# A fused attention and two-layer kernel on one core: the rational function's denominator moves from POOL to ACT and DVE, and the second token block goes from f32 to three f16 passes

## The chip, the cores and the metric

The kernel runs on one core of one Trainium2 chip. Its time is the device time of one execution in microseconds (us), and smaller is better. Five engines work side by side, each through its own instruction queue in order, and wait for each other by semaphores: PE (matrix multiply; its weight loads are shown apart as PEld), DVE (vector), ACT (activation functions), POOL (the general-purpose engine), and SP, which here issues all transfers. A measurement of this kernel can tell about 1% from no change.

## The reference

Three stages follow each other on 4608 tokens (8 batches of 576):

```
p_packed = softmax(p k^T / 8) v          # 32 packed rows a head, 8 heads of 64
x        = softmax(q p_packed^T / 8) p_packed
h = x @ w_in                             # 512 -> 2048
P = a0 + a1 h + a2 h^2 + a3 h^3
Q = 1 + |b0| |h| + |b1| h^2
y = (P / (Q + 1e-6)) @ w_out             # 2048 -> 512
h2 = y @ w_in2                           # 512 -> 1024
solu = h2 * softmax(h2)
out = ((solu - mean) / sqrt(var + 1e-6) * g_ln) @ w_out2
```

All is in f32. The four weights come as 64-bit floats, 25 MB, and are turned into f32 on the chip with integer operations on DVE.

## The kernel before, in words

The tokens are worked off in 9 blocks of 512. For each block there are 16 steps i, one for each 128 of the 2048 hidden columns:

- `m_h` multiplies on PE into one of two PSUM banks (tile `h`). Attention is folded in: `a_pw` makes `pw` (packed rows times w_in) once a batch, and `m_h` multiplies the attention weights `at` with it.
- `elem` (line 678) computes the rational function of that bank. ACT takes |h| into `u` (L690). POOL makes `s` = b1 u + b0 (L335, called at L691), and then `s` = s u (L692); that is the denominator without its 1. ACT makes the numerator's inner part `B` (L693), DVE goes on with it (L694, L695; both read `h` in PSUM). ACT takes Ln and Exp of the denominator (L696, L697), which gives its reciprocal, and DVE does one Newton step and the product (L698, L699, L701 or L703; all their inputs are in SBUF).
- `m_y` multiplies the result `g` with w_out into `Y`, four PSUM banks (tiles `P`).

After the 16 steps `y_out` evicts Y as two f16 halves into `ybig` (ACT L728, DVE L729), twice 128x1024. Then for each quarter t of the block `s_h2` multiplies with w_in2, `s_sm`, `s_lt` and `s_ln` do softmax, transposes by DMA and statistics, and `s_out` multiplies with w_out2.

Precision has two forms. A plain f32 matmul, or both operands split into a high and a low f16 part and three f16 matmuls (`PASS`, line 659) accumulated. `NRAW = 2` (line 204): the first two blocks' `m_y` and the first two batches' `m_h` are f32; the others are in three f16 passes. With f16, `elem` ends in one more step: ACT casts `g`'s high part (L704) and POOL subtracts for the low part (L705). `w_split` (line 454) turns w_out, w_in2 and w_out2 into two f16 parts in place: ACT the high part (L457), DVE the low part (L458). Since the f32 form reads w_out in place, its splits follow block 1's `m_y`, the last that needs f32.

Early on the weights must also be loaded and decoded (`w_decode`, three DVE operations a piece, L399 to L401, 24 pieces), and column sums give bounds that set the f16 scales (`w_bound`, `w_scale`, and `a_scale`, a chain of some 30 one-column operations, mostly on POOL, for each block).

The order on each engine is written by a planner (`Plan`). Every operation has a due time, 16 a block plus an entry of the table `DUE`, and a cost; a list scheduler goes through time with these costs and puts on each engine the earliest due operation that is ready. On the chip nothing is left of the plan but the order on each queue and the semaphores. Buffers are few: 3 each of `s`, `u`, `B` and `g`, 2 banks of `h`, and one PSUM pair that `s_h2`, `a_pw` and the attention share.

## Time and profile before

| | |
|---|---|
| time, median of 3 runs | 1197.74 us (1196.11 to 1203.66) |
| the profiled execution | 1202.27 us, its span 1200.4 us |
| PE busy | 1115.8 us (93%) |
| DVE busy | 976.8 us (81%) |
| ACT busy | 762.0 us (63%) |
| POOL busy | 706.3 us (59%) |
| mean granted clock of PE | 0.983 |

Busy is the time in which at least one instruction of the engine runs. Matmuls overlap each other and their ends are modelled, so how fast PE goes is read from the distance of their starts. A line can be a helper's: every matmul is recorded at L329 and every POOL operation on one tensor at L335, so they are told apart by their tiles. An f32 matmul stands in the trace as two records.

### The profile page before, as it was taken

The page shows a single profiled execution, that of the slowest core. Times are in us where ns is not written, and L with a number is a line of the kernel's source. Part 1 is how long each engine was busy: PE and PEld are TensorE (multiplying, and loading weights), DVE is VectorE, ACT ScalarE, POOL GpSimd, SP SyncE. Part 2 cuts the span into 40 slices and gives each one's busy share as a digit, 9 for nine tenths or more (in the row PEclk, how much of TensorE's full clock was granted, in tenths as well). Part 3 has the DMA queues.
Part 4 walks back from the last instruction along what each step waited for, and adds up shares of the span by engine and source line. Part 5 has one row for each costly group of instructions (what it writes and reads, how often), then busy time and mean ns, then how long its engine had stood idle before and what let it go on. Part 6 is the DMA issues. An engine that isn't in the chain of part 4 may idle for free.

```text
span 1200.4 us, 17951 instructions
## 1 busy us (share of the span) xinstructions
PE 1115.8 (93%) x6549; PEld 529.7 (44%) x6550; DVE 976.8 (81%) x1477; ACT 762.0 (63%) x1256; POOL 706.3 (59%) x931
## 2 busy tenths in 40 slices
PE   4678989999999999999999998999999999999998
PEld 1133344444444454444544454444444444444443
DVE  5987999999978978888878887888788886788633
ACT  3556666676856667567756766577656666667624
POOL 0163847554658647676666655765675865867612
PEclk9698999999999999999999999999999999999999
DMA  9664033110222121311231114111311121211123
GB/s 342 224 230 161 7 123 99 36 53 1 54 77 67 27 54 55 88 27 28 62 109 27 27 40 131 27 27 27 117 28 27 27 53 28 53 27 27 27 53 88
DMA packets 108120, 83.54 MB, mean 70 GB/s; under 512 B 78208, under 2 KB 88576, under 8 KB 108032
## 3 DMA queue, kind: packets, MB, share of 16 engines
q1 hardware_dynamic: 108032, 82.40, 24.4%
q8 instruction: 51, 0.84, 0.3%
q14 instruction: 37, 0.30, 0.1%
HBM read 54.07 MB, written 9.44 MB: 53 GB/s over the span
## 4 chain that ended last, share of the span: by engine, by line
PE 47%; DVE 23%; POOL 13%; ACT 9%; issue 5%; DMA 2%; SPq 0%; DVEq 0%; ACTq 0%; POOLq 0%
PE P L329 37%; PE h L329 9%; POOL s L692 4%; POOL cf L335 3%; DVE B L699 3%; POOL s L335 2%; DVE s L698 2%; POOL g L705 2%; ACT u L696 2%; DVE B L694 2%; DVE B L695 2%; POOL d L335 1%; DVE w L401 1%; DMA lbig<-lbig 1%; DVE at L629 1%
## 5 line engine op out<-in xcount | busy, mean ns | idle before, releaser
L329 PE MATMUL P<-g,w 128*128 128x512 f16 (+1 forms) x1600 | 423.4, 414 | 0.7 <-DVE ybig L729 0.7
L329 PE MATMUL h<-at,pw 128*128 128x192 f16 (+11 forms) x1408 | 235.4, 315 | 8.3 <-ACT at L646 3.2
L335 POOL TENSOR_SCALAR s<-u,aba 128x512 f32<-128x512 f32 x130 | 137.6, 1058 | 173.7 <-ACT u L690 150.9
L329 PEld LDWEIGHTS <-w 128*128 128x128 f16 x1440 | 138.4, 98 | 167.5 <-issue 12.1
L329 PE MATMUL P<-w,ybig 128*128 128x512 f16 x864 | 193.9, 381 | 9.0 <-DVE pw L539 2.5
L705 POOL TENSOR_TENSOR g<-B,g 128x512 f16<-128x512 f32 x112 | 144.2, 1287 | 80.9 <-ACT g L704 76.6
L692 POOL TENSOR_TENSOR s<-s,u 128x512 f32<-128x512 f32 x130 | 186.3, 1433 | 7.0
L329 PE MATMUL P<-w,lbig 128*128 128x512 f16 x768 | 173.0, 379 | 4.9 <-DVE pw L539 2.9
L335 POOL TENSOR_SCALAR d<-d 128x1 f32<-128x1 f32 x216 | 85.3, 395 | 156.6 <-ACT E L790 73.1
L696 ACT ACTIVATE u<-s,lnb 128x512 f32<-128x512 f32 x130 | 93.8, 721 | 98.4 <-POOL s L692 97.9
L698 DVE SCALAR_TENSOR_TENSOR s<-s,u 128x512 f32<-128x512 f32 x130 | 109.2, 840 | 47.8 <-ACT u L697 47.0
L329 PEld LDWEIGHTS <-ybig 128*128 128x128 f16 x864 | 84.7, 98 | 114.2 <-issue 16.0
L329 PEld LDWEIGHTS <-pw 128*128 128x128 f16 x1152 | 101.6, 98 | 64.5 <-issue 13.3
L329 PEld LDWEIGHTS <-lbig 128*128 128x128 f16 x768 | 74.6, 98 | 92.6 <-issue 8.1
L694 DVE SCALAR_TENSOR_TENSOR B<-h,cf,B 128x512 f32<-128x512 f32 x112 | 83.0, 741 | 27.5 <-ACT B L693 27.3
L693 ACT ACTIVATE B<-h,cf 128x512 f32<-128x512 f32 x112 | 86.6, 773 | 21.5 <-POOL g L705 21.5
L699 DVE SCALAR_TENSOR_TENSOR B<-B,cf,u 128x512 f32<-128x512 f32 x101 | 98.2, 972 | 0.0
L697 ACT ACTIVATE u<-u,lnb 128x512 f32<-128x512 f32 x133 | 95.6, 719 | 2.0
L690 ACT ACTIVATE u<-h,cf 128x512 f32<-128x512 f32 x101 | 68.9, 682 | 39.9 <-PE h L329 38.1
L695 DVE SCALAR_TENSOR_TENSOR B<-B,cf,h 128x512 f32<-128x512 f32 x112 | 82.8, 739 | 1.5
L704 ACT CAST g<-B 128x512 f16<-128x512 f32 x112 | 68.6, 613 | 21.6 <-PE P L329 16.9
L703 DVE SCALAR_TENSOR_TENSOR B<-s,B 128x512 f32<-128x512 f32 x98 | 81.0, 827 | 1.1
(144 smaller groups left out, 1469.3 us busy)
## 6 DMA issues: line engine op xcount, KB each, us to landing
w<-in_w_in_dram SPq DMA_DIRECT2D x10, 1024.0 KB, 9.2
kq<-in_kT_dram SPq DMA_DIRECT2D x8, 1152.0 KB, 6.2
w<-in_w_out_dram SPq DMA_DIRECT2D x9, 1024.0 KB, 8.1
kq<-in_qT_dram SPq DMA_DIRECT2D x9, 1024.0 KB, 5.4
out_dram<-w SPq DMA_DIRECT2D x36, 256.0 KB, 2.4
...
```

The source lines that it names most:

```text
L329: nc.tensor.matmul(out=o, lhsT=lhsT, rhs=rhs, start=start, stop=stop)
L335: gp.tensor_scalar(out=o, in0=i, scalar1=s1, scalar2=s2, op0=o0, **({"op1": o1} if o1 else {}))
L692: pool(due, c_pool(512, 2), lambda: gp.tensor_tensor(out=T(s_), in0=T(s_), in1=T(u_), op=ALU.mult), [u_, s_], [s_])
L693: sc(due, c_act(512, 163), lambda: act.activation(out=T(B_), in_=T(h_), func=AF.Identity, scale=coef(17), bias=coef(16)), [h_, *R], [B_], ...
L694: dve(due, c_dve(512), lambda: stt(out=T(B_), in0=T(h_), scalar=coef(14), in1=T(B_), op0=ALU.mult, op1=ALU.mult), [h_, B_, *R], [B_])
L695: dve(due, c_dve(512), lambda: stt(out=T(B_), in0=T(B_), scalar=coef(15), in1=T(h_), op0=ALU.subtract, op1=ALU.mult), [h_, B_, *R], [B_])
L696: sc(due, c_act(512, 105), lambda: act.activation(out=T(u_), in_=T(s_), func=AF.Ln, scale=2.0 ** -40, bias=lnb[:, 0:1]), [s_, "lnb"], [u_])
L697: sc(due, c_act(512, 105), lambda: act.activation(out=T(u_), in_=T(u_), func=AF.Exp, scale=-1.0, bias=lnb[:, 1:2]), [u_, "lnb"], [u_])
L698: dve(due, c_dve(512, 140), lambda: stt(out=T(s_), in0=T(s_), scalar=1.0 + 1e-6, in1=T(u_), op0=ALU.add, op1=ALU.mult), [s_, u_], [s_])
L699: dve(due, c_dve(512, 240), lambda: stt(out=T(B_), in0=T(B_), scalar=coef(18), in1=T(u_), op0=ALU.subtract, op1=ALU.mult), [B_, u_, *R], [B_])
L703: dve(due, c_dve(512, 95), lambda: stt(out=T(B_), in0=T(s_), scalar=2.0, in1=T(B_), op0=ALU.subtract, op1=ALU.mult), [s_, B_], [B_])
L705: pool(due, (1250, 1290), lambda: gp.tensor_tensor(out=T(g_)[:, 1, :], in0=T(B_), in1=T(g_)[:, 0, :], op=ALU.subtract), [B_, g_], [g_])
```

## The change

- `elem`: the denominator no longer goes through POOL. ACT squares h into `s` (scaled by the block's factor, coefficient 14) and takes |h| times b0 into `u` (a new coefficient 22, made by one more one-column POOL operation a block from block 1 on), and DVE joins them: s = b1 s + u, both inputs in SBUF. The old way stays in the code behind `Q_POOL`, which is false for all blocks.
- `NRAW` is 1: block 1, and the second batch, go in three f16 passes. So block 1's `elem` has the cast on ACT and the subtraction on POOL (`LO_POOL` is true throughout), the second batch's `pw` and `at` are split, and w_out's 16 splits follow block 0's `m_y`.
- `w_split` of w_out: ACT makes the high part and then scales the f32 row in place, and POOL subtracts (`LOW_POOL`); DVE has no part in it. The other two weights are split as before.
- The planner: other costs, a rule that DVE operations marked `port` aren't planned beside a POOL operation, and a new table `DUE` with entries for single weight pieces and for blocks 0, 1 and 8. Nothing of these three is executed, but they set the order.

```diff
-    NRAW = 2
+    NRAW = 1
+    LOW_POOL = {1: 1, 2: 0, 3: 0}
+    Q_POOL = lambda j, i: False
+    LO_POOL = lambda j, i: True
...
         sc(due, c_act(512, 100), lambda: act.activation(out=spl[w][:, c, 0, :], in_=raw[w][:, c + 1, :], func=AF.Copy, scale=s), [b, ("wst", w)], [a])
+        if LOW_POOL[w]:
+            sc(due, c_act(512, 100), lambda: act.activation(out=raw[w][:, c + 1, :], in_=raw[w][:, c + 1, :], func=AF.Copy, scale=s), [b, ("wst", w), a], [b])
+            pool(due, (1117, 1157), lambda: gp.tensor_tensor(out=spl[w][:, c, 1, :], in0=raw[w][:, c + 1, :], in1=spl[w][:, c, 0, :], op=ALU.subtract), [a, b], [a, ("spl", w, c)])
+            return
...
-        sc(due, c_act(512, 65), lambda: act.activation(out=T(u_), in_=T(h_), func=AF.Abs, scale=coef(14)), [h_, *R], [u_], [(u_, "u"), (s_, "s")])
-        pool(due, c_pool(512), lambda: ps_(T(s_), T(u_), aba[:, 5:6], aba[:, 4:5], ALU.mult, ALU.add), [u_, "ab"], [s_])
-        pool(due, c_pool(512, 2), lambda: gp.tensor_tensor(out=T(s_), in0=T(s_), in1=T(u_), op=ALU.mult), [u_, s_], [s_])
...
+            sc(due, c_act(512, 65), lambda: act.activation(out=T(s_), in_=T(h_), func=AF.Square, scale=coef(14)), [h_, *R], [s_], [(s_, "s")])
+            sc(due, c_act(512, 65), lambda: act.activation(out=T(u_), in_=T(h_), func=AF.Abs, scale=coef(22)), [h_, *R], [u_], [(u_, "u")])
+            dve(due, c_dve(512), lambda: stt(out=T(s_), in0=T(s_), scalar=aba[:, 5:6], in1=T(u_), op0=ALU.mult, op1=ALU.add), [u_, s_, "ab"], [s_], port=True)
...
+                        if n in self.port and port_at > now:
+                            held.append((due, n))
+                            continue
```

Two places show how the order moves. The first is POOL's queue from its first operation on data, in block 0 of the program. Before, it begins with the denominators of the first steps (L335 and L692 in turn; `aba` holds |a| and |b|):

```order
L335 TENSOR_SCALAR s_85<-u_87,aba 128x512
L692 TENSOR_TENSOR s_85<-s_85,u_87 128x512
L335 TENSOR_SCALAR s_86<-u_88,aba 128x512
L692 TENSOR_TENSOR s_86<-s_86,u_88 128x512
L335 TENSOR_SCALAR s_85<-u_87,aba 128x512
L692 TENSOR_TENSOR s_85<-s_85,u_87 128x512
```

Now it begins with the scale of w_out, the first split of w_out (L483) and the chain of block 0's coefficients:

```order
L358 TENSOR_SCALAR wst<-wst 128x1 x2
L483 TENSOR_TENSOR w_75<-w_75 128x512
L358 TENSOR_SCALAR wst<-wst 128x1 x2
L358 TENSOR_SCALAR cf_117<-pmx 128x1
L358 TENSOR_SCALAR cf_117<-cf_117,wst 128x1
L358 TENSOR_SCALAR cf_117<-cf_117,aba 128x1 x2
```

No denominator is left on POOL; `w_75` is w_out.

The second place is DVE around the second eviction of Y (block 1's, into `ybig`). The rows with `cf_119` are elementwise work of block 2 that stands ahead of it or around it (`cf_118` holds block 1's coefficients). Before:

```order
L698 SCALAR_TENSOR_TENSOR s_85<-s_85,u_87 128x512
L458 SCALAR_TENSOR_TENSOR w_75<-w_75,wst 128x512
L699 SCALAR_TENSOR_TENSOR B_89<-B_89,cf_119,u_87 128x512
L703 SCALAR_TENSOR_TENSOR B_89<-s_85,B_89 128x512
L694 SCALAR_TENSOR_TENSOR B_90<-h_83,cf_119,B_90 128x512
L695 SCALAR_TENSOR_TENSOR B_90<-B_90,cf_119,h_83 128x512
L729 SCALAR_TENSOR_TENSOR ybig<-P_80,cf_118,ybig 128x2x512
L729 SCALAR_TENSOR_TENSOR ybig<-P_81,cf_118,ybig 128x2x512
```

Now (L725 is the join, L765 the eviction):

```order
L728 SCALAR_TENSOR_TENSOR B_90<-B_90,cf_119,h_84 128x512
L731 SCALAR_TENSOR_TENSOR s_85<-s_85,u_87 128x512
L732 SCALAR_TENSOR_TENSOR B_89<-B_89,cf_119,u_87 128x512
L725 SCALAR_TENSOR_TENSOR w_75<-w_75,aba,w_76 128x512
L736 SCALAR_TENSOR_TENSOR B_89<-s_85,B_89 128x512
L731 SCALAR_TENSOR_TENSOR s_86<-s_86,u_88 128x512
L765 SCALAR_TENSOR_TENSOR ybig<-P_80,cf_118,ybig 128x2x512
L765 SCALAR_TENSOR_TENSOR ybig<-P_81,cf_118,ybig 128x2x512
```

Ahead of this eviction stood 22 operations of block 2's `elem` on DVE, and now 11 stand there, three of them joins; the splits of w_out (L458), of which one shows there, are on POOL now. On PE the work ahead of it is the same in both, but for three steps of block 2's `m_h` in place of five.

## Rows read from the trace of the kernel before

**Rows 1.** The profile's page: the span, and the busy time, share of the span and instructions of each engine.

```profile
span 1200.4 us, 17951 instructions
PE 1115.8 (93%) x6549; PEld 529.7 (44%) x6550; DVE 976.8 (81%) x1477; ACT 762.0 (63%) x1256; POOL 706.3 (59%) x931
```

**Rows 2.** The view by windows, five stages of the span: the length, the busy time of each engine (with instructions), the granted clock of PE, the share of the DMA engines, GB/s.

```profile
0.00:120.00 120.00, 80.90 (x487) 31.98 (x489) 93.41 (x136) 63.98 (x122) 35.07 (x25) 0.86 0.68 239
120.00:198.00 78.00, 70.87 (x372) 30.36 (x372) 74.59 (x115) 51.13 (x92) 50.71 (x62) 0.98 0.25 80
198.00:331.00 133.00, 129.88 (x534) 61.71 (x533) 128.15 (x196) 94.09 (x157) 75.35 (x93) 1.00 0.14 38
331.00:990.00 659.00, 627.43 (x4174) 311.38 (x4173) 545.98 (x831) 430.32 (x691) 430.92 (x599) 1.00 0.21 52
990.00:1200.00 210.00, 206.70 (x988) 94.33 (x986) 134.70 (x202) 122.46 (x197) 114.27 (x155) 1.00 0.20 43
```

**Rows 3.** The timeline of DVE at the first and the second eviction of Y: start in us, duration in us, engine, line, operation, tiles, count.

```profile
195.77 2.48 DVE L729 SCALAR_TENSOR_TENSOR ybig<-P,cf,ybig 128x1024 f16<-128x1024 f32 x2 [0.30 <-ACT ybig L728]
...
328.80 2.47 DVE L729 SCALAR_TENSOR_TENSOR ybig<-P,cf,ybig 128x1024 f16<-128x1024 f32 x2
```

**Rows 4.** The timeline of PE in two stretches without idle time: block 1 with f32 (`P<-g,w` is `m_y`, the `h` row is two steps of `m_h`), and a later one with f16 (`P<-w,lbig` is the last multiply, of the same shape as `m_y`).

```profile
261.53 7.13 PE L329 MATMUL P<-g,w 128*128 128x512 f32 x16
268.50 7.03 PE L329 MATMUL P<-w,E 128*128 128x512 f32 x16
275.37 4.17 PE L329 MATMUL h<-at,pw 128*128 128x64 f32 x16
279.38 3.60 PE L329 MATMUL P<-g,w 128*128 128x512 f32 x8
...
415.42 5.34 PE L329 MATMUL P<-w,lbig 128*128 128x512 f16 x24
420.59 1.47 PE L329 MATMUL h<-at,pw 128*128 128x192 f16 x12
```

**Rows 5.** The groups of DVE's instructions from 0 to 331 us, shapes apart: count, busy us, mean ns of one, idle us before them and what ended it.

```profile
L699 DVE SCALAR_TENSOR_TENSOR B<-B,abc,u 128x512 f32<-128x512 f32 x32 | 29.1, 910 | 0.0
L458 DVE SCALAR_TENSOR_TENSOR w<-w,wst 128x512 f16<-128x512 f32 x32 | 26.8, 843 | 0.0
L701 DVE SCALAR_TENSOR_TENSOR g<-s,B 128x512 f32<-128x512 f32 x32 | 22.7, 709 | 0.0
L539 DVE SCALAR_TENSOR_TENSOR pw<-P,bnd,pw 128x1024 f16<-128x1024 f32 x4 | 5.1, 1278 | 0.5 <-ACT pw L538 0.5
```

**Rows 6.** The timelines of DVE and POOL in two stretches of block 8's elementwise work: in the first POOL works on two tensors, in the second its timeline shows nothing from 1063.9 to 1069.5 us.

```profile
1048.56 0.68 DVE L698 SCALAR_TENSOR_TENSOR s<-s,u 128x512 f32<-128x512 f32 x1
1049.16 1.75 DVE L699 SCALAR_TENSOR_TENSOR B<-B,cf,u 128x512 f32<-128x512 f32 x1
...
1048.70 1.66 POOL L692 TENSOR_TENSOR w<-w,u 128x512 f32<-128x512 f32 x1
...
1067.18 0.74 DVE L699 SCALAR_TENSOR_TENSOR B<-B,cf,u 128x512 f32<-128x512 f32 x1
1067.96 0.68 DVE L703 SCALAR_TENSOR_TENSOR B<-s,B 128x512 f32<-128x512 f32 x1
```

**Rows 7.** The timeline of all engines in block 0 (idle time before an instruction, and what ended it, in brackets).

```profile
77.41 10.88 POOL L335 TENSOR_SCALAR s<-u,aba 128x512 f32<-128x512 f32 x1 [3.73 <-DVE g L701]
...
89.67 0.72 ACT L696 ACTIVATE u<-s,lnb 128x512 f32<-128x512 f32 x1 [10.12 <-POOL s L692]
...
93.13 0.59 PE L329 MATMUL P<-w,ones 128*32 128x512 bf16 x1 [9.54 <-ACT pw L534]
...
96.35 0.28 DVE L332 TENSOR_SCALAR p<-P,sum 128x64 f32<-128x64 f32 x1 [8.02 <-PE P L329]
```

**Rows 8.** Groups of the whole span, from the profile's page, with the same columns as rows 5: what POOL does in `elem`, and ACT's |h|.

```profile
L335 POOL TENSOR_SCALAR s<-u,aba 128x512 f32<-128x512 f32 x130 | 137.6, 1058 | 173.7 <-ACT u L690 150.9
L705 POOL TENSOR_TENSOR g<-B,g 128x512 f16<-128x512 f32 x112 | 144.2, 1287 | 80.9 <-ACT g L704 76.6
L692 POOL TENSOR_TENSOR s<-s,u 128x512 f32<-128x512 f32 x130 | 186.3, 1433 | 7.0
L690 ACT ACTIVATE u<-h,cf 128x512 f32<-128x512 f32 x101 | 68.9, 682 | 39.9 <-PE h L329 38.1
```

**Rows 9.** The groups of DVE's instructions from 331 to 990 us.

```profile
L699 DVE SCALAR_TENSOR_TENSOR B<-B,cf,u 128x512 f32<-128x512 f32 x76 | 73.3, 965 | 0.0
L698 DVE SCALAR_TENSOR_TENSOR s<-s,u 128x512 f32<-128x512 f32 x75 | 66.0, 880 | 28.1 <-ACT u L697 28.0
L694 DVE SCALAR_TENSOR_TENSOR B<-h,cf,B 128x512 f32<-128x512 f32 x86 | 63.7, 740 | 19.6 <-ACT B L693 19.4
L757 DVE SCALAR_TENSOR_TENSOR E<-P,d,E 128x1024 f32<-128x1024 f32 x22 | 28.1, 1279 | 16.6 <-ACT E L752 16.5
L750 DVE TENSOR_REDUCE d<-P 128x1 f32<-128x1024 f32 x22 | 26.8, 1218 | 10.2 <-PE P L329 10.2
```

**Rows 10.** The groups of PE's instructions from 331 to 990 us.

```profile
L329 PE MATMUL P<-g,w 128*128 128x512 f16 x1032 | 236.8, 379 | 0.2 <-DVE ybig L729 0.2
L329 PE MATMUL P<-w,ybig 128*128 128x512 f16 x538 | 121.5, 382 | 7.2 <-DVE at L627 2.3 <-DVE pw L539 2.3 <-DVE p L332 1.4
L329 PE MATMUL P<-w,lbig 128*128 128x512 f16 x528 | 119.4, 379 | 4.9 <-DVE pw L539 2.9 <-DVE E L757 1.2 <-DVE pmx L359 0.4
```

More of the change, by code (lines that the diff above doesn't have):

```diff
@@ L50, in __init__, with add @@
         self.parts, self.last_w, self.readers, self.users, self.kind, self.place = [], {}, {}, {}, {}, {}
-        self.slots, self.held, self.pace = {}, {}, {}
+        self.slots, self.held, self.pace, self.port = {}, {}, {}, set()
     def hold(self, key, slot):
         self.kind[key], self.held[key] = None, slot
-    def add(self, eng, due, cost, fn, r=(), w=(), new=(), pace=None):
+    def add(self, eng, due, cost, fn, r=(), w=(), new=(), pace=None, port=False):
         n = len(self.parts)
+        if port or eng == "POOL":
+            self.port.add(n)
         if pace is not None:
@@ L100, in order @@
                 heapq.heappush(ready[p[0]], (p[1], n))
-        out, now, events, pace = [], 0.0, [], 0.0
+        out, now, events, pace, port_at = [], 0.0, [], 0.0, 0.0
         bytes_free = 0.0
@@ L138, in order @@
                     free_at[eng] = now + occ
+                    if got in self.port:
+                        port_at = now + occ
                     if eng == "SP":
@@ L299, in c_pool @@
     def c_pool(n, tensors=1):
-        lat = (2.4 * n + 220) if tensors > 1 else (1.3 * n + 330)
+        lat = (2.14 * n + 175) if tensors > 1 else (0.94 * n + 290)
         return lat - 40, lat
@@ L314, in pe, with dve @@
         plan.add("PE", due, c_pe(mms), run, r, w, new, pace)
-    def dve(due, cost, fn, r=(), w=(), new=()):
-        plan.add("DVE", due, cost, fn, r, w, new)
+    def dve(due, cost, fn, r=(), w=(), new=(), port=False):
+        plan.add("DVE", due, cost, fn, r, w, new, port=port)
     def sc(due, cost, fn, r=(), w=(), new=()):
@@ L398, in w_decode @@
         ov = flat(o.bitcast(U32))
-        dve(due, c_dve2(1024), lambda: v_.tensor_scalar(out=ov, in0=H, scalar1=3, scalar2=0x3FFFFFFF, op0=ALU.logical_shift_left, op1=ALU.bitwise_and), keys, ok)
-        dve(due, c_dve(1024, 0), lambda: v_.scalar_tensor_tensor(out=ov, in0=L, scalar=29, in1=ov, op0=ALU.logical_shift_right, op1=ALU.bitwise_or), keys + ok, ok)
-        dve(due, c_dve(1024, 0), lambda: v_.scalar_tensor_tensor(out=ov, in0=H, scalar=0xC0000000, in1=ov, op0=ALU.bitwise_and, op1=ALU.bitwise_or), keys + ok, ok)
+        dve(due, c_dve2(1024), lambda: v_.tensor_scalar(out=ov, in0=H, scalar1=3, scalar2=0x3FFFFFFF, op0=ALU.logical_shift_left, op1=ALU.bitwise_and), keys, ok, port=True)
+        dve(due, c_dve(1024, 0), lambda: v_.scalar_tensor_tensor(out=ov, in0=L, scalar=29, in1=ov, op0=ALU.logical_shift_right, op1=ALU.bitwise_or), keys + ok, ok, port=True)
+        dve(due, c_dve(1024, 0), lambda: v_.scalar_tensor_tensor(out=ov, in0=H, scalar=0xC0000000, in1=ov, op0=ALU.bitwise_and, op1=ALU.bitwise_or), keys + ok, ok, port=True)
         a = t.bitcast(BF16)
@@ L628, in a_s2 @@
         dve(d, c_dve(1024, 0), lambda: v_.tensor_reduce(out=rA(), in_=X3(), axis=AX.X, op=ALU.max), [x_], [rk], [(rk, "r32")])
-        dve(d, c_dve(1024, 0), lambda: v_.tensor_tensor(out=X3(), in0=X3(), in1=bc(rA()), op=ALU.subtract), [x_, rk], [x_])
+        dve(d, c_dve(1024, 0), lambda: v_.tensor_tensor(out=X3(), in0=X3(), in1=bc(rA()), op=ALU.subtract), [x_, rk], [x_], port=True)
         sc(d, c_act(1024, 0), lambda: act.activation(out=X(), in_=X(), func=AF.Exp, scale=0.125), [x_], [x_])
@@ L639, in a_s2 @@
         dve(d, (262, 344), lambda: v_.reciprocal(out=rB(), in_=rB()), [rk], [rk])
-        dve(d, c_dve(1024, 0), lambda: v_.tensor_tensor(out=X3(), in0=X3(), in1=bc(rB()), op=ALU.mult), [x_, rk], [x_])
+        dve(d, c_dve(1024, 0), lambda: v_.tensor_tensor(out=X3(), in0=X3(), in1=bc(rB()), op=ALU.mult), [x_, rk], [x_], port=True)
         dve(d, c_dve(1024, 20), lambda: v_.transpose(out=T(yk), in_=X()), [x_], [yk], [(yk, "E")])
@@ L649, in a_s2 @@
                 dve(d, c_dve(2 * n, 0), lambda a=a, t=t, n=n: v_.tensor_tensor(out=a()[:, 1, :, :], in0=Y()[:, :, t:t + n], in1=a()[:, 0, :, :], op=ALU.subtract),
-                    [yk, ("a", j, t)], [x_, ("a", j, t)])
+                    [yk, ("a", j, t)], [x_, ("a", j, t)], port=True)
     def piece(j, t, n, b):
@@ L774, in s_lt @@
         sc(due, c_act(1024, 20), lambda: act.activation(out=l[:, 0, 0, :], in_=T(E), func=AF.Copy, scale=2.0 ** 13), [E], [R, *old])
-        dve(due, c_dve(1024, 0), lambda: v_.scalar_tensor_tensor(out=l[:, 0, 1, :], in0=T(E), scalar=2.0 ** 13, in1=l[:, 0, 0, :], op0=ALU.mult, op1=ALU.subtract), [E, R], [(R, 1)])
+        dve(due, c_dve(1024, 0), lambda: v_.scalar_tensor_tensor(out=l[:, 0, 1, :], in0=T(E), scalar=2.0 ** 13, in1=l[:, 0, 0, :], op0=ALU.mult, op1=ALU.subtract), [E, R], [(R, 1)], port=True)
         for a in range(2):
```

33 lines of the change are left out of this document (21 added, 12 removed), and 20 rows, old and new, of the table DUE.

## The prediction

> **What bounds the kernel now.** I read the page first, then the windows, then DVE's and PE's timelines where the windows change. On the page PE is busy for 93% of the span and DVE for 81% [rows 1], which hides that two stages have different limits. In the windows [rows 2] PE has 39.1 us of idle time before 120 us (120 less 80.90), 7.1 and 3.1 in the next two stages, 31.6 from 331 to 990, and 3.3 in the last 210 us. DVE is the other way round: from 120 to 331 us it works 202.7 of 211 us, from 331 to 990 it has 113 us to spare. So from about 20 us to 331 us the weights' decoding and two blocks' elementwise work keep **DVE** at its limit, and afterwards **PE** sets the time. The seam is the second eviction of Y, which ends at 331.3 us [rows 3]; 869.1 us of the span follow it.
>
> The span is 1200.4 us, the profiled execution 1202.27, the median of the runs 1197.74. My sums are differences against the profiled span, and I take them off the median.
>
> **PE's saving.** f32 `m_y` in block 1: 16 records take 268.50 - 261.53 = 6.97 us, so one step (8 records, 4 matmuls) takes 3.49 us. In f16, 24 matmuls take 420.59 - 415.42 = 5.17 us, so 12 take 2.59 [rows 4]. That saves 0.90 x 16 = 14.4 us. Two f32 steps of `m_h` take 279.38 - 275.37 = 4.01 us; six f16 passes of 512 columns take 1.29 us by the same row, and 1.5 with the 64 columns of block 1 that stay f32. That saves 0.5 x 16 = 8.0. Together **22 us of PE work**, all ahead of the seam, where DVE is the limit. Behind the seam PE's work is the same but for two steps of `m_h` more: the order puts three ahead of the eviction in place of five, +2.6 us.
>
> **DVE up to the seam.** It was busy for 93.41 + 74.59 + 128.15 = 296.2 us and idle for 34.8 [rows 2]. Instructions that follow each other overlap by 0.08 us (1048.56 + 0.68 against the next start at 1049.16 [rows 6]), so I take 0.08 off each duration.
> - The join reads two tensors in SBUF, as L701 does (mean 709 ns [rows 5]); undisturbed, L703 takes 0.68 [rows 6]. I take 0.62 us, since L701 ran in the same blocks: 32 x 0.62 = +19.8. The upper end is L699's mean of 965 [rows 9], 0.885: +28.3.
> - w_out's splits leave DVE: 16 x (0.843 - 0.08) [rows 5] = -12.2.
> - The second batch's `pw` gets its low part on DVE: 4 x (1.278 - 0.08) [rows 5] = +4.8. The low part of `at` for 896 columns of block 1 and 256 of block 2, by L701's rate: +1.4. Five more one-column operations for block 1's scales, at most 0.28 each (the row at 96.35 [rows 7]): +1.
> - The order: 22 operations of block 2 stood ahead of the eviction, 11 do now. By L694 (0.740 - 0.08 [rows 9]): -7.3.
> - Idle time. At 77.41 a POOL operation of a denominator took 10.88 us, while DVE ran on; ACT then waited 10.12 us for POOL, PE 9.54 us for ACT, and DVE at last 8.02 us for PE [rows 7]. With no denominator on POOL this chain is gone: -8. I add -2 for the smaller waits of the same kind, by judgement.
> - The port. DVE's work on two SBUF tensors grows when POOL works on two tensors at the same time: L699 took 1.75 us with L692 beside it and 0.74 with POOL idle [rows 6]. L692 goes, but 16 splits of w_out and 16 low parts of block 1 come to POOL, also on two tensors. That is 32 for the 37 steps that had run, so I take -1. The Trainium skill (GPSIMD Engine Reference, Specifications) says that POOL shares its SBUF interfaces with VectorE and that DVE instructions with two SBUF inputs contend; L699's two rows agree, and by the rule alone every join would count at the disturbed 0.885, which makes the sum below +5.0 in place of -3.5.
>
> Sum: 19.8 - 12.2 + 4.8 + 1.4 + 1 - 7.3 - 10 - 1 = **-3.5 us**. So the seam moves little, and most of PE's 22 us become idle time. ACT doesn't decide: it was busy 209 of 331 us, and gets 32 squares of at most 0.682 [rows 8] and some 32 operations for casts and splits, together 44 us.
>
> **Behind the seam.** Here PE sets the time, and `m_y` never waits for `g` (0.2 us in 1032 matmuls [rows 10]). So a shorter chain in `elem` (two ACT operations and a join in place of one and two on POOL of 1.06 and 1.43 us [rows 8]) gives nothing by itself. What PE waits for is DVE, late with `pw`, `at`, `E` and small columns, in 12.1 us of the two groups shown and 31.6 us in all. DVE gets 86 joins (as many as L694 has rows [rows 9]): +53. It loses waiting behind POOL's L692: of POOL's 112 + 130 operations on two tensors on the page [rows 8] the 130 go, about half; L699's excess is 76 x (0.965 - 0.74) = 17 us and L698's 75 x (0.88 - 0.68) = 15, and with L703's a little less I take 23 us back. So DVE goes from 546 to 576 of 659 us, 87%: no limit on average. For PE I take 10 of its 35 us of idle time as won, between nothing and 20: the stretched operations stand in the chains that PE waits for (L629, L649 and L699 all read two SBUF tensors), and POOL comes to the short operations of the statistics sooner. This is the least certain term, and the +2.6 above is set against the waits that a PE two steps behind no longer has.
>
> Forecast: 1197.7 - 3.5 - 10 = **1184 us**.
>
> **The rivals.**
> *A, PE's saving comes through.* DVE's idle time up to the seam shrinks from 34.8 to the 12 or so of the first transfers, because many of its small waits hung on POOL, and the new order fills them; then the seam comes up to 22 us earlier, and behind it the 10 us are won: 1198 - 32 = 1166. For it: DVE's first 120 us hold 26.6 of its idle time, of which the chain at 77 us explains only 8. Against it: DVE had 8.3 us idle in the 211 us after, so it must be the early part alone.
>
> *B, the port takes it back.* In the first two blocks DVE works without a gap, and POOL's splits and low parts meet it; the joins cost 0.885, and the new POOL operations are held up as the one at 77.41 was, now ahead of `m_y` of block 1, which didn't need POOL before. Joins +8.5, no idle time won +10, no gain behind the seam +10: 1184 + 28 = 1212, or 1203 if only the joins and the gain behind the seam fail. For it: 1.75 us of L699 beside L692 against 0.74 without [rows 6]. Against it: POOL's work on two tensors falls by half, and L701 kept 709 ns in these blocks.
>
> *C, DVE becomes the limit behind the seam.* It has 113 us to spare in 659, but 28.1 of it are waits of L698 for ACT, 19.6 of L694, 16.6 of L757, 10.2 of L750 [rows 9], together 74.5. If these stay, only 38.5 us are free, 0.45 us for each of 86 steps; from there on each further 0.1 us a step costs 8.6 us. I have 0.62 a join less 23/86 = 0.27 won back, 0.35, which is under it. At 0.885 with nothing won back it is 0.435 over: 86 x 0.435 = 37 us, 1198 - 3.5 + 37 = 1232, slower. For it: the join stands in DVE's queue between two operations that wait for ACT. Against it: waits shrink when an engine gets fuller, and ACT no longer waits for POOL.
>
> *D, the change doesn't reach POOL.* It does: the order has no denominator there.
>
> **The numbers.** Forecast 0.50, from 1174 to 1197; A 0.24; B 0.16; C 0.10. Under 1% is what a measurement here can't tell from no change, so faster means below 1185.8 and slower above 1209.7. Of the forecast I give 0.28 to faster and 0.22 to no change; A is faster; B gives 0.11 to no change and 0.05 to slower; C is slower. So faster 0.52, no change 0.33, slower 0.15. The range from 1162 to 1208 leaves out C, half of B's upper value and the lowest part of A.
>
> **What will show it.** Right: the second eviction of Y ends between 318 and 331 us; PE's idle time ahead of it is longer by some 18 us; POOL is busy for about 390 us (706 less 359 of denominators, 1.433 + 1.058 for each of 144 steps, plus 32 x 1.29 [rows 8]); the join's mean lies between 0.69 and 0.80 us; PE's idle time behind the seam falls to about 25 us. A is right if the eviction ends before 312; B if the join's mean is above 0.9 or a POOL split is held for over 3 us and PE waits for it; C if DVE is busy for over 92% from the seam to 990 us and PE waits for `g`. I am wrong in principle if the time changes without the seam or PE's idle time behind it having moved.

## The result, and the profile after

The changed kernel takes **1162.94 us** (median of 4 runs, 1162.42 to 1163.76) against 1200.2 us for the kernel before in the same measurement: ratio 0.9691, 95% interval 0.9654 to 0.9728. That is 37 us faster, where 14 were forecast. The profiled execution took 1162.42 us, its span is 1160.6. One execution each of a1_old_plan and a2_old_ops below took far longer than the rest, 2932.52 and 1953.92 us; without it their medians are 1232.64 and 1183.46.

The page's span and busy line, and the view by windows for the stretches that answer to [rows 1, 2] (the seam now lies at 318 us):

```profile
span 1160.6 us, 18141 instructions
PE 1090.8 (94%) x6678; PEld 519.6 (45%) x6678; DVE 1002.0 (86%) x1616; ACT 851.1 (73%) x1432; POOL 418.7 (36%) x696
...
0.00:120.00 120.00, 82.04 (x537) 31.43 (x538) 102.76 (x160) 77.38 (x143) 19.64 (x40) 0.90 0.67 239
120.00:198.00 78.00, 65.33 (x342) 29.01 (x340) 76.93 (x116) 68.03 (x121) 30.54 (x31) 0.95 0.20 72
198.00:318.00 120.00, 113.64 (x596) 54.82 (x597) 115.00 (x189) 96.73 (x164) 53.98 (x80) 0.98 0.17 46
318.00:950.00 632.00, 623.86 (x4205) 310.37 (x4202) 555.52 (x912) 472.26 (x781) 248.51 (x429) 1.00 0.23 56
950.00:1160.00 210.00, 205.90 (x1006) 93.94 (x1004) 151.75 (x244) 136.69 (x226) 66.01 (x118) 1.00 0.21 40
```

DVE's timeline at the second eviction of Y, to be held against [rows 3]:

```profile
314.53 0.68 DVE L731 SCALAR_TENSOR_TENSOR s<-s,u 128x512 f32<-128x512 f32 x1
315.13 2.47 DVE L765 SCALAR_TENSOR_TENSOR ybig<-P,cf,ybig 128x1024 f16<-128x1024 f32 x2
```

It ends at 317.6 us in place of 331.3, so 13.7 us are won ahead of the seam. From there to the end of the span it is 843.0 in place of 869.1: **26.1 us are won behind it**. PE's idle time behind the seam is 8.1 + 4.1 = 12.2 us by the windows; before it was 31.6 + 3.3 = 34.9. So nearly all of what was won there is time in which PE had waited.

What PE waited for shows in the view of waits (engine, tile and line that waited, what it waited for; us in total, times, longest). Before, from 331 to 990 us:

```profile
PE P L329 <- DVE E L757: 5.7, 4, 2.8
PE P L518 <- DVE p L332: 5.7, 5, 1.6
PE P L329 <- DVE pw L539: 5.2, 6, 2.0
...
PE P L329 <- DVE at L627: 2.3, 1, 2.3
PE h L329 <- DVE at L649: 2.1, 2, 1.6
```

After, from 318 to 950 us:

```profile
PE P L545 <- DVE p L355: 2.3, 5, 0.7
...
PE P L352 <- DVE E L793: 1.4, 4, 0.5
```

It is DVE's lateness that went, although DVE is busy for more of the time (1002.0 us in all against 976.8). The groups of DVE from 318 to 950 us, with the columns of [rows 9], tell how: its idle time ahead of operations that wait for ACT shrank. L731 (before L698) waits 11.6 us in place of 28.1, L727 (before L694) 1.1 in place of 19.6, and the join L725 adds 4.5.

```profile
L732 DVE SCALAR_TENSOR_TENSOR B<-B,cf,u 128x512 f32<-128x512 f32 x87 | 67.4, 774 | 0.0
L731 DVE SCALAR_TENSOR_TENSOR s<-s,u 128x512 f32<-128x512 f32 x82 | 66.4, 810 | 11.6 <-ACT u L730 10.5
...
L727 DVE SCALAR_TENSOR_TENSOR B<-h,cf,B 128x512 f32<-128x512 f32 x87 | 64.6, 742 | 1.1 <-ACT B L726 0.9
L725 DVE SCALAR_TENSOR_TENSOR s<-s,aba,u 128x512 f32<-128x512 f32 x82 | 62.2, 759 | 4.5 <-ACT u L724 4.4
```

And the page's chain of waits (shares of the span by engine) had POOL in it before, and has no longer:

```profile
PE 47%; DVE 23%; POOL 13%; ACT 9%; issue 5%; DMA 2%; SPq 0%; DVEq 0%; ACTq 0%; POOLq 0%
```

```profile
PE 54%; DVE 33%; ACT 8%; issue 3%; POOL 1%; DMA 1%; ACTq 0%; DVEq 0%; POOLq 0%
```

The first is before, the second after. 13% of 1200 us are 156 us, of which the page's next line gives the denominators (L692 and L335) 4% and 2%.

### The profile page after: what moved, and what is told of

It reads as the page before. It is cut to its first block, busy times and chain, and to the rows that moved or that the text cites. A ratio compares the mean times of both kernels' runs of the same rounds, so it can differ in the third digit from the quotient of the medians.

```text
span 1160.6 us, 18141 instructions
## 1 busy us (share of the span) xinstructions
PE 1090.8 (94%) x6678; PEld 519.6 (45%) x6678; DVE 1002.0 (86%) x1616; ACT 851.1 (73%) x1432; POOL 418.7 (36%) x696
## 4 chain that ended last, share of the span: by engine, by line
PE 54%; DVE 33%; ACT 8%; issue 3%; POOL 1%; DMA 1%; ACTq 0%; DVEq 0%; POOLq 0%
PE P L352 42%; PE h L352 11%; DVE B L732 3%; DVE s L731 3%; DVE B L727 3%; DVE B L728 3%; DVE B L736 2%; DVE s L725 2%; DVE w L423 2%; DVE w L424 1%; DVE d L786 1%; DVE pw L566 1%; DVE w L485 1%; DVE w L422 1%; DVE E L793 1%
## 5 line engine op out<-in xcount | busy, mean ns | idle before, releaser
L739 POOL TENSOR_TENSOR g<-B,g 128x512 f16<-128x512 f32 x128 | 158.1, 1235 | 252.0 <-ACT g L737 242.7
L352 PE MATMUL h<-at,pw 128*128 128x448 f16 (+8 forms) x1472 | 230.4, 305 | 17.1 <-DVE B L728 13.4
L352 PEld LDWEIGHTS <-w 128*128 128x128 f16 x1632 | 158.4, 98 | 187.0 <-issue 11.6
L352 PEld LDWEIGHTS <-pw 128*128 128x128 f16 x1344 | 115.9, 99 | 79.4 <-issue 21.8
L723 ACT ACTIVATE s<-h,cf 128x512 f32<-128x512 f32 x114 | 77.9, 684 | 51.3 <-PE h L352 51.1
L731 DVE SCALAR_TENSOR_TENSOR s<-s,u 128x512 f32<-128x512 f32 x127 | 100.3, 790 | 17.6 <-ACT u L730 16.5
L725 DVE SCALAR_TENSOR_TENSOR s<-s,aba,u 128x512 f32<-128x512 f32 x127 | 97.0, 764 | 7.8 <-ACT u L724 7.7
L726 ACT ACTIVATE B<-h,cf 128x512 f32<-128x512 f32 x128 | 100.0, 781 | 0.7 <-PE h L352 0.7
L727 DVE SCALAR_TENSOR_TENSOR B<-h,cf,B 128x512 f32<-128x512 f32 x128 | 94.9, 742 | 2.0 <-ACT B L726 1.6
L728 DVE SCALAR_TENSOR_TENSOR B<-B,cf,h 128x512 f32<-128x512 f32 x128 | 94.7, 741 | 2.2
L732 DVE SCALAR_TENSOR_TENSOR B<-B,cf,u 128x512 f32<-128x512 f32 x123 | 95.8, 780 | 0.0
L724 ACT ACTIVATE u<-h,cf 128x512 f32<-128x512 f32 x123 | 84.1, 683 | 0.9 <-DVE B L732 0.9
L736 DVE SCALAR_TENSOR_TENSOR B<-s,B 128x512 f32<-128x512 f32 x114 | 78.7, 690 | 1.2
```

The source lines that it names most:

```text
L352: nc.tensor.matmul(out=o, lhsT=lhsT, rhs=rhs, start=start, stop=stop)
L725: dve(due, c_dve(512), lambda: stt(out=T(s_), in0=T(s_), scalar=aba[:, 5:6], in1=T(u_), op0=ALU.mult, op1=ALU.add), [u_, s_, "ab"], [s_], ...
L726: sc(due, c_act(512, 163), lambda: act.activation(out=T(B_), in_=T(h_), func=AF.Identity, scale=coef(17), bias=coef(16)), [h_, *R], [B_], ...
L727: dve(due, c_dve(512), lambda: stt(out=T(B_), in0=T(h_), scalar=coef(14), in1=T(B_), op0=ALU.mult, op1=ALU.mult), [h_, B_, *R], [B_])
L728: dve(due, c_dve(512), lambda: stt(out=T(B_), in0=T(B_), scalar=coef(15), in1=T(h_), op0=ALU.subtract, op1=ALU.mult), [h_, B_, *R], [B_])
L731: dve(due, c_dve(512, 0), lambda: stt(out=T(s_), in0=T(s_), scalar=1.0 + 1e-6, in1=T(u_), op0=ALU.add, op1=ALU.mult), [s_, u_], [s_], port ...
```

## The experiments

Three causes could stand behind the 37 us: the new order, the new operations through the **port** (short for POOL's and DVE's operations stretching each other, as in [rows 6]), and the new operations through the **chain** of each step (ACT, POOL, ACT, DVE before; ACT, DVE, ACT, DVE now). Every ratio is against the kernel before on the same chip, which took 1199 to 1203 us. The first kernels are planned anew, so that every queue changes; later ones keep the changed kernel's order and alter one thing in it.

### Order against operations

**a1_old_plan**: the change's operations with before's table, costs and no port rule (look-ahead 16).

```diff
-        lat = (2.14 * n + 175) if tensors > 1 else (0.94 * n + 290)
+        lat = (2.4 * n + 220) if tensors > 1 else (1.3 * n + 330)
...
-        if port or eng == "POOL":
-            self.port.add(n)
```

> The changed kernel's operations, ordered by the planner of before (its table of due times, its costs, no port rule; the look-ahead is 16 in place of 14.05, with which no order is found). Theory 1 (POOL's withdrawal makes DVE's work shorter, and PE stops waiting for DVE): the gain stays without the new order, 1163 to 1172 us, PE idle from the second eviction to the end under 18 us. Theory 2 (the new order does it): 1185 to 1200 us, PE idle there 30 us or more.

1233.84 us, ratio 1.0274 (1.0221 to 1.0327): slower than before.

**a2_old_ops**: before's operations, planned with the change's table, costs and rule.

```diff
-    NRAW = 1
-    LOW_POOL = {1: 1, 2: 0, 3: 0}
-    Q_POOL = lambda j, i: False
+    NRAW = 2
+    LOW_POOL = {1: 0, 2: 0, 3: 0}
+    Q_POOL = lambda j, i: True
```

> The operations of before (denominators and two f32 blocks as before, w_out's splits on DVE), ordered by the changed planner with its table, costs and port rule. Theory 1: 1190 to 1205 us, PE idle behind the second eviction stays near 35 us. Theory 2: 1170 to 1180 us, PE idle there 12 to 20 us.

1184.18 us, ratio 0.9858 (0.9807 to 0.9909).

**a3_pool_denoms**: the changed kernel with the denominators of blocks 2 to 8 back on POOL, planned anew.

```diff
-    Q_POOL = lambda j, i: False
+    Q_POOL = lambda j, i: j >= 2
```

> The changed kernel with the denominators of blocks 2 to 8 back on POOL (|h| on ACT, two operations on POOL, no join); blocks 0 and 1 and the planner unchanged. Theory 1: 20 to 26 us of the gain are lost, 1183 to 1190 us, L699's counterpart back at 0.95 us or more in the mean. Theory 2: 1163 to 1168 us.

1175.92 us, ratio 0.9793 (0.9744 to 0.9843). DVE is busy for only 961.9 us there and the kernel is still 13 us slower than with 1002.0. ACT's Ln shows why (groups of ACT: first this kernel from 329 to 961 us, then the changed kernel from 318 to 950):

```profile
L729 ACT ACTIVATE u<-s,lnb 128x512 f32<-128x512 f32 x67 | 48.3, 720 | 42.8 <-POOL s L721 42.6
```

```profile
L729 ACT ACTIVATE u<-s,lnb 128x512 f32<-128x512 f32 x82 | 59.4, 725 | 20.0 <-DVE s L725 19.4
```

**a4_nraw2**: the changed kernel with `NRAW = 2`, so block 1 in f32.

```diff
-    NRAW = 1
+    NRAW = 2
```

> The changed kernel with block 1 in f32 again (and the second batch's products), all else as changed; w_out's splits move behind block 1's multiply. If DVE sets the time up to the second eviction, as I read it, PE's 22 us more are mostly hidden: 1163 to 1172 us. If PE's saving came through (rival A): 1180 to 1190 us.

1164.16 us, ratio 0.9699 (0.9659 to 0.974). Block 1 in f16 is worth about 1 us, no more than can be told from nothing.

So the parts don't add. By their ratios, of 1200 us, the new planning alone gives 17 us, the new operations alone cost 33, and both together give 37.

The second eviction is not the same point in every order, since different shares of block 2 stand ahead of it. The third and the eighth lie where all these kernels work in f16, with about the same work of PE between them (it is busy for 575 to 583 us). DVE's timeline there, two rows each of the kernel before, the changed kernel and a3_pool_denoms:

```profile
451.16 2.48 DVE L729 SCALAR_TENSOR_TENSOR ybig<-P,cf,ybig 128x1024 f16<-128x1024 f32 x2 [0.24 <-ACT ybig L728]
...
1057.21 2.46 DVE L729 SCALAR_TENSOR_TENSOR ybig<-P,cf,ybig 128x1024 f16<-128x1024 f32 x2
```

```profile
437.80 2.47 DVE L765 SCALAR_TENSOR_TENSOR ybig<-P,cf,ybig 128x1024 f16<-128x1024 f32 x2 [0.65 <-ACT ybig L764]
...
1019.67 2.46 DVE L765 SCALAR_TENSOR_TENSOR ybig<-P,cf,ybig 128x1024 f16<-128x1024 f32 x2
```

```profile
431.46 2.48 DVE L765 SCALAR_TENSOR_TENSOR ybig<-P,cf,ybig 128x1024 f16<-128x1024 f32 x2
...
1032.91 2.46 DVE L765 SCALAR_TENSOR_TENSOR ybig<-P,cf,ybig 128x1024 f16<-128x1024 f32 x2
```

These five blocks take 606.0 us before, 581.9 in the changed kernel and 601.4 in a3_pool_denoms; in a2_old_ops they take 600.7. So 24 of the 37 us lie here. With the changed planner and denominators on POOL only about 5 of them come; the other 19 to 20 come when the denominators leave POOL, although DVE works 27 us more in the stretch then (513.4 us against 486.5 in a3_pool_denoms). That a3_pool_denoms loses only 13 us in all is because it reaches the third eviction 6 us earlier than the changed kernel. With before's planner the withdrawal does not pay: in a1_old_plan the same stretch takes about 628 us.

The next three ask which part of the planning it is.

**e_table_only**: the change's table, but before's costs and no rule (the diff of a1_old_plan, with the table kept).

> The changed kernel's operations with its table of due times, but the planner has the costs of before and no port rule. With the table, the costs and the rule of before the same operations took 1233.84 us, with those of the change 1162.94. If the table of due times alone carries the order, 1160 to 1175 us; if the costs or the rule matter, 1190 to 1235; in between they share it. The place to look is the first eviction of Y (227.6 us in the old order, 190.2 in the new) and the time from the third eviction to the end (771.3 and 720.3).

1210.47 us, ratio 1.0091 (1.006 to 1.0121).

**f_costs_only**: before's table with look-ahead 16, the change's costs, no rule. With the table come its entries for weight pieces:

```diff
-            w_load(w, g, at(0, f"L{w}{g}"), places.get((w, g), lstage))
+            w_load(w, g, at(0, f"L{w}", g), places.get((w, g), lstage))
...
-        if port or eng == "POOL":
-            self.port.add(n)
```

> The changed kernel's operations with before's table of due times (look-ahead 16, as in the run that took 1233.84 us) and no port rule, but with the change's costs for POOL, for small operations and for lines 731, 732 and 736. It completes a square: table old or new, costs old or new, of which old/old is 1233.84 and new/old 1210.47. If table and costs add up, it lies below 1233.84 by as much as the run with the new table, new costs and no rule lies below 1210.47; if the costs matter only together with the table that was made for them, 1225 to 1240.

1242.43 us, ratio 1.0335 (1.0297 to 1.0374).

**b3_no_port_rule**: the change's table and costs, no rule.

```diff
-        if port or eng == "POOL":
-            self.port.add(n)
```

> The changed kernel, its table and its costs, planned without the rule that DVE's port operations are not planned beside a POOL operation. Together with before's costs this took 1210.47 us. If the rule carries the order: 1190 to 1215. If the costs do: 1160 to 1172, and the rule is worth nothing, since what the planner thinks to be simultaneous is not so on the chip.

1204.58 us, ratio 1.0038 (1.0013 to 1.0063). The same operations take 1163 to 1242 us in these orders; the costs by themselves don't help with the old table, and without the rule the table loses 42 us. Where a poor order loses is seen at the join, in the groups of DVE of a1_old_plan (460 to 1000 us) and b3_no_port_rule (318 to 950):

```profile
L711 DVE SCALAR_TENSOR_TENSOR s<-s,aba,u 128x512 f32<-128x512 f32 x59 | 43.9, 743 | 31.6 <-ACT u L710 31.4
```

```profile
L723 DVE SCALAR_TENSOR_TENSOR s<-s,aba,u 128x512 f32<-128x512 f32 x80 | 61.0, 763 | 17.9 <-ACT u L722 17.7
```

In the changed kernel the join waits 4.5 us. Placed too early in DVE's queue it stands waiting for ACT's |h|, and all behind it waits too. These runs don't say whether the rule is good in itself: the table may only fit the planner that it was made with.

### The port, at a fixed order

**b2_one_tensor**: the kernel before in its own order, L692 reads one tensor.

```diff
-        pool(due, c_pool(512, 2), lambda: gp.tensor_tensor(out=T(s_), in0=T(s_), in1=T(u_), op=ALU.mult), [u_, s_], [s_])
+        pool(due, c_pool(512, 2), lambda: gp.tensor_scalar(out=T(s_), in0=T(s_), scalar1=1.0, scalar2=None, op0=ALU.mult), [u_, s_], [s_])
```

> The kernel before in its own order; POOL's second operation of a denominator multiplies s by 1 in place of by u, so that it reads one tensor. It leaves out the factor u of the denominator's second-order term. All else is the same, instruction by instruction. Theory P: L699's mean from 331 to 990 us falls from 965 ns to below 850 and L698's from 880 to below 780, DVE loses 20 to 30 us, and the time falls to 1183 to 1192, which is half or more of the 20 us that the changed denominators gave with the new order. Theory C: POOL's operation gets shorter by 0.4 us at most, the chain stays, the time is 1194 to 1202.

1192.71 us, ratio 0.9929 (0.9907 to 0.9952). DVE is busy for 938.3 us, 38.5 less than before, and the time falls by 8. So DVE was stretched. That the time fell by so little does not show that DVE had room, for the edit has a second side: L692 got longer, not shorter (a mean of 1605 ns from 331 to 990 us in place of 1379), and ACT's Ln waited 54.0 us for it in place of 43.6. L699 stays at 896 ns (965 before): beside POOL's operations on one tensor alone it took a mean of 807 ns (41 times), with none beside it 743 (33 times). So an operation on one tensor stretches DVE too, if less.

**b1_two** and **b1_one**: the changed kernel in its own order, with POOL's subtraction done twice from block 2 on, or preceded by an operation on one tensor. Of the second edit, as of those of d1, d2 and c2 below, only the added part is shown.

```diff
-            pool(due, (1117, 1157), lambda: gp.tensor_tensor(out=T(g_)[:, 1, :], in0=T(B_), in1=T(g_)[:, 0, :], op=ALU.subtract), [B_, g_], [g_])
+            pool(due, (1117, 1157), lambda: [gp.tensor_tensor(out=T(g_)[:, 1, :], in0=T(B_), in1=T(g_)[:, 0, :], op=ALU.subtract) for _ in range(2 if j >= 2 else 1)], [B_, g_], [g_])
```

```diff
+ gp.tensor_scalar(out=T(g_)[:, 1, :], in0=T(B_), scalar1=1.0, scalar2=None, op0=ALU.mult) if j >= 2 else None
```

> The changed kernel in its own order; from block 2 on POOL does its subtraction for the low part of g twice (the same values, the same output), so 112 operations on two tensors of about 1.2 us come to POOL, with no new operation on DVE and none elsewhere. Theory P (the port: the denominators cost time on POOL because POOL's work on two tensors stretches DVE's): DVE's two-tensor operations in elem (lines 725 to 736 of the changed kernel, 683 to 810 ns from 318 to 950 us) grow by 0.1 us or more each, DVE is busier by 25 to 45 us, and the time is 1170 to 1185. Theory C (the chain: what cost time was that POOL sat between ACT and DVE): this only puts 1.2 us behind each step, between g's parts and a multiply that does not wait for g; DVE's means stay, the time is 1161 to 1168.

1202.39 us, ratio 1.0008 (0.9987 to 1.0029).

> As the run with the doubled subtraction, but POOL's additional operation reads one tensor (a multiply of B by 1 into the same place, then the subtraction), of about 1 us, 112 times. Theory P: POOL is busy as long, but DVE's means stay within 0.03 us of the changed kernel, and the time is 1161 to 1167, 8 us or more below the run with two tensors. Theory C: the same time as the run with two tensors, within 4 us, whichever that is. If both are slower than 1170, what costs is POOL's time itself: its queue, and so the short operations of the statistics that wait in it.

1184.91 us, ratio 0.9863 (0.9822 to 0.9903). Both are above 1170, the case that the expectation put down to POOL's own time, and they lie 17 us apart. DVE's L732 tells of the port, from 318 to 950 us, first with one tensor, then with two (774 ns without):

```profile
L732 DVE SCALAR_TENSOR_TENSOR B<-B,cf,u 128x512 f32<-128x512 f32 x84 | 73.1, 870 | 0.0
```

```profile
L732 DVE SCALAR_TENSOR_TENSOR B<-B,cf,u 128x512 f32<-128x512 f32 x82 | 79.4, 968 | 0.0
```

The operations that read `h` in PSUM stay at 742 to 743 ns in both. The Trainium skill (GPSIMD Engine Reference, Specifications) names DVE instructions with two SBUF inputs among those that contend with POOL; with that the trace agrees. The 870 ns of b1_one are not the added operation's own doing: all 13 of L732's executions over 850 ns there ran beside the subtraction on two tensors, which the added operation had moved against L732.

That leaves whether DVE's time or POOL's costs. **d1_dve_load** gives DVE one more operation a step, **d2_pool_memset** gives POOL two that only write:

```diff
+ v_.tensor_scalar(out=T(u_)[:, :320], in0=T(u_)[:, :320], scalar1=1.0, scalar2=None, op0=ALU.mult) if j >= 2 else None
```

```diff
+ [gp.memset(T(g_)[:, 1, :], 0.0) for _ in range(2)] if j >= 2 else None
```

> The changed kernel in its own order; from block 2 on DVE does one more operation a step on a buffer that nobody reads any more (u times 1 in place, 320 columns, one tensor in SBUF), 112 times, after the operation of line 732. POOL and ACT get nothing. With POOL's one-tensor operation doubled instead, DVE's busy time grew by 34.5 us through slower operations and the time by 22 us. Theory D (behind the seam DVE's own time costs, whoever lengthens it): this adds 25 to 45 us to DVE's busy time, and the time grows by half to all of that, to 1175 to 1200. Theory Q (POOL's queue costs: the short operations of the statistics wait in it, and PE waits for what follows from them): DVE has room (76 us of 632 idle), 1162 to 1169.

1179.91 us, ratio 0.9818 (0.9776 to 0.986).

> The changed kernel in its own order; from block 2 on POOL fills the place of g's low part with zeros twice before it subtracts, 112 times, which reads no tensor at all. Theory Q: POOL is busy for 60 to 150 us more, and the time grows as it did with the one-tensor operation, in the proportion of the busy time that comes to POOL (0.11 us for each us there: 202 us busy, 22 us slower): 1170 to 1180. Theory D: the time grows only as far as DVE's busy time does; if writes alone do not slow DVE, 1161 to 1168.

1172.86 us, ratio 0.976 (0.9725 to 0.9795). The busy lines of these two pages, d1 first:

```profile
PE 1092.1 (93%) x6677; PEld 517.5 (44%) x6678; DVE 1034.9 (88%) x1728; ACT 853.8 (72%) x1432; POOL 414.7 (35%) x696
```

```profile
PE 1096.6 (94%) x6677; PEld 521.1 (44%) x6678; DVE 1018.8 (87%) x1616; ACT 852.7 (73%) x1432; POOL 549.7 (47%) x920
```

| against the changed kernel | DVE busy, us | POOL busy, us | span, us |
|---|---|---|---|
| d1_dve_load | +32.9 | -4.0 | +17.8 |
| d2_pool_memset | +16.8 | +131.0 | +10.5 |
| b1_one | +34.5 | +202.0 | +22.1 |
| b1_two | +57.9 | +176.1 | +39.4 |

d1_dve_load is the clean one: POOL does no more, and each microsecond added to DVE, between L732 and L736 of each step, costs 17.8 / 32.9 = 0.54 behind the seam, although DVE has 76 us idle in 632 there. Between the two b1 kernels, DVE's 23.4 us more come with 17.3 us of span, while POOL is busy for 26 us less. In d2_pool_memset and b1_one the two can't be told apart: by c2_beside below POOL's own time can cost up to 0.11 us for each, which is 14 and 22 us, as much as their whole losses. So the price of DVE's time rests on d1_dve_load and on the difference of the b1 kernels.

### The chain, at a fixed order

By that price the change should have lost behind the seam, since DVE is busier there than before, by 27 us. So the chain was tried by itself. **c2_chain**: three one-column operations on POOL between the join and Ln. **c2_beside**: the same three behind L732, where nobody waits for them but the next user of the buffer. The edits, in the join's line and in L732's:

```diff
+ [ps_(T(s_)[:, :1], T(s_)[:, :1], 1.0, None, ALU.mult) for _ in range(3 if j >= 2 else 0)]
```

```diff
+ [ps_(T(u_)[:, :1], T(u_)[:, :1], 1.0, None, ALU.mult) for _ in range(3 if j >= 2 else 0)]
```

> The changed kernel in its own order; from block 2 on three one-column operations on POOL (about 0.35 us each) stand between the join and ACT's Ln, 112 times, on one column of s (times 1). DVE and ACT get nothing to do. This makes the chain of each step longer by some 1.3 us and the waits behind POOL's other work, without data to speak of. Theory C (the chain counts, because DVE's queue is in order: what stands behind an operation that waits for ACT is late too, up to E and pw for which PE waits): DVE's busy time stays within 5 us of 1002, its idle time ahead of line 731 grows, and the time is 1170 to 1185. Theory D (only DVE's busy time counts, and g has slack): 1160 to 1166.

1210.53 us, ratio 1.0079 (1.005 to 1.0108).

> The changed kernel in its own order with the same three one-column operations on POOL 112 times, but on one column of u after its last use (behind line 732), so that nobody waits for them but the next user of that buffer. Theory C: 5 us or more below the run with them in the chain, 1162 to 1169. Theory Q (POOL's queue itself costs): the same time as in the chain, within 3 us.

1174.35 us, ratio 0.9782 (0.9729 to 0.9836). The same work costs 48 us in the chain and 11 beside it. DVE is busy for 1003.7 and 999.2 us, as in the changed kernel (1002.0). So POOL's queue costs at most 11 us for 104 us of work (522.9 busy against 418.7), 0.11 for each, and the rest of the 48, **36 us, is the place in the chain**. What grew in the chain are waits, in the groups from 318 to 950 us (DVE's L731, POOL's three operations, ACT's Ln):

```profile
L731 DVE SCALAR_TENSOR_TENSOR s<-s,u 128x512 f32<-128x512 f32 x76 | 61.1, 804 | 49.1 <-ACT u L730 39.2 <-ACT d L830 3.7 <-issue 2.6
...
L358 POOL TENSOR_SCALAR s<-s 128x1 f32<-128x1 f32 x231 | 68.3, 296 | 170.0 <-DVE s L725 155.3 <-DVE nb L355 1.6
...
L729 ACT ACTIVATE u<-s,lnb 128x512 f32<-128x512 f32 x77 | 55.7, 723 | 84.4 <-POOL s L358 55.5 <-DVE B L727 26.3 <-DVE B L728 2.3
```

The three operations take 3 x 0.296 = 0.89 us a step. ACT waits for them (55.5 of its 84.4 us), DVE waits at L731 for ACT (49.1 us in place of 11.6), and what stands behind in the queues is late for PE, though `g` is not. The view of PE's waits from 318 to 950 us:

```profile
PE P L352 <- DVE E L793: 9.8, 10, 1.5
PE P L352 <- ACT w L848: 8.7, 9, 1.7
PE P L352 <- ACT E L528: 3.6, 4, 1.5
PE P L352 <- ACT E L517: 3.6, 3, 1.6
```

**c3_pool_join**: the join itself on POOL, in two operations.

```diff
-            dve(due, c_dve(512), lambda: stt(out=T(s_), in0=T(s_), scalar=aba[:, 5:6], in1=T(u_), op0=ALU.mult, op1=ALU.add), [u_, s_, "ab"], [s_], port=True)
+            dve(due, c_dve(512), lambda: [ps_(T(s_), T(s_), aba[:, 5:6], None, ALU.mult), gp.tensor_tensor(out=T(s_), in0=T(s_), in1=T(u_), op=ALU.add)] if j >= 2 else stt(out=T(s_), in0=T(s_), scalar=aba[:, 5:6], in1=T(u_), op0=ALU.mult, op1=ALU.add), [u_, s_, "ab"], [s_], port=True)
```

> The changed kernel in its own order; from block 2 on the join is made on POOL in two operations (s times b1, then s plus u) in place of one on DVE. So DVE loses 112 joins, some 80 us, and POOL gains about 270 us of work, as before the change, with nothing planned anew. By DVE's busy time alone (0.6 us each) the time would fall to the floor that PE sets, 1150 to 1160; with the port's stretch of DVE's other operations taken into account DVE still loses 40 us, 1150 to 1163. Theory C: the chain is longer by 2 us and more a step, so DVE and ACT wait in it, and the time is 1175 to 1200, at or above the 1175.92 of the same work in an order planned for it.

1275.87 us, ratio 1.0631 (1.0579 to 1.0682). DVE is busy for 974.0 us, 28 less, and the time is 113 us longer; ACT's Ln waits 113.4 us for POOL from 318 to 950. The forecast by DVE's busy time fails altogether. a3_pool_denoms, planned for POOL's denominators, lost only 13, so I read most of the 113 us as an order that doesn't know of the longer chain. PE's granted clock may have a share too: it was 0.95 in the mean from 318 to 950 us, 1.00 in the changed kernel. The 113 us were not taken apart further.

Of the fifteen times of this section nine lie outside every range that was stated for them: a1, a2, a3, b2, b1_two, f, c2_chain, c2_beside and c3. So what tells the causes apart is which of two kernels is slower and what the traces show of their waits; the sizes were mostly not foreseen.

## Why the prediction was wrong

**The step that failed** is that a shorter chain in `elem` "gives nothing by itself", and with it the term "10 of its 35 us of idle time as won". The premise was true and stayed true: the groups of PE after show no wait of `m_y` for `g`.

```profile
L352 PE MATMUL P<-g,w 128*128 128x512 f16 x1032 | 236.8, 379 | 0.0
```

But it was the wrong place to look. DVE's and ACT's queues are in order, so an operation of `elem` that waits there holds up E, pw and at behind it, and for those PE does wait. c2_chain shows it at a fixed order. The term was mis-sized at -10; it measured -26.1, most of it (24.2) from the third to the eighth eviction, and there about 5 come with the new planning alone and the other 19 to 20 with the denominators' leaving POOL. The page had the sign of it: POOL's 13% in the chain of waits, and 43.6 us of ACT's Ln waiting for POOL from 331 to 990 us, which the prediction didn't use:

```profile
L696 ACT ACTIVATE u<-s,lnb 128x512 f32<-128x512 f32 x74 | 53.4, 722 | 43.9 <-POOL s L692 43.6
```

**The seam** came 13.7 us earlier in place of 3.5; it lies at 317.6, just under the 318 that were given. DVE's idle time up to it fell by 34.8 - 23.3 = 11.5, and 10 were forecast: that step holds, and POOL's stall at 77 us is gone with its cause (POOL's first operation now starts at 94.09 us). DVE's busy time went from 296.2 to 294.7 where the sum had +6.5. The joins cost more than 19.8: L725's four groups up to the seam hold 21.4 + 4.8 + 2.2 + 0.8 = 29.2 us for 35 joins (three of them block 2's), 26.4 after the overlap. What was too small is the port, put at -1. Three groups of DVE up to 317.6 us, for [rows 5]'s L699 (910 ns) and L458 (843 ns), and for one of the two decoding operations on `w`, which took 1291 ns before:

```profile
L423 DVE SCALAR_TENSOR_TENSOR w<-w,w 128x1024 uint32<-128x1024 uint32 x18 | 22.0, 1220 | 0.1
...
L732 DVE SCALAR_TENSOR_TENSOR B<-B,abc,u 128x512 f32<-128x512 f32 x16 | 12.8, 798 | 0.0
...
L485 DVE SCALAR_TENSOR_TENSOR w<-w,wst 128x512 f16<-128x512 f32 x16 | 11.8, 739 | 0.0
```

In all their groups up to the seam, line 732's operation took 26.1 us for 34 in place of 32.1 for 36 (-4.2 at equal count), the two decoding operations 58.5 in place of 62.3 (-3.8), and the 16 splits that stayed 0.1 us less each (-1.7): -9.7. I had counted POOL's operations on two tensors (32 for 37) as if the number decided; that the new order keeps them apart from DVE's I had not looked at, and it is not shown here either. The joins' +6.6 and the port's -8.7 beyond the forecast make -2.1 of the -8.0 by which DVE's busy time came out lower; the remaining 6 us are spread over small groups and stay open.

**PE's 22 us** were hidden, as said: with block 1 in f32 (a4_nraw2) the kernel takes 1.2 us more, and its second eviction ends only 5.2 us later, with 21 us more of PE's work ahead of it. PE's idle time ahead of the seam is 7.7 us longer, not 18, since the seam itself moved by 13.7; together 21.4.

**DVE behind the seam**: 576 of 659 us, 87%, was forecast; it is 555.5 of 632, 88%. The join's mean is 0.764 us on the page, inside 0.69 to 0.80. POOL is busy for 419 us, not 390: the subtraction costs 128 x 1.235 = 158 us as expected, and POOL's one-column operations make up the rest (239 us in place of 211).

**The rivals.** *A* gave the nearest time, 1166, but not by its reason: it wanted the seam before 312 us. *B* is out: joins at 0.764, PE doesn't wait for a split. *C* named a mechanism that exists (d1_dve_load), but with the wrong form. There is no reserve of 38.5 us behind which DVE's time begins to cost; 32.9 us of it already cost 17.8. What kept C from coming is that the waits it took as fixed at 74.5 us fell: by the groups they are 11.6 + 1.1 + 4.5 for L731, L727 and the join, and 15.5 and 16.2 for L793 and L786 (before L757 and L750), 48.9 together. *D* is out.

**What stays open.** How much of the whole 37 us belongs to the order and how much to the operations has no single answer, since they don't add: the 19 to 20 us above hold for the changed planner, and with before's planner the same withdrawal cost time. Why just this order serves this chain was not taken apart further than the join's place, and that the port's relief ahead of the seam comes from the order is not shown.
